# A fused mLSTM, soft mixture and routed mixture: a new order of the opening, three routed tiles planned early instead of two, and a new order between the mixtures

## The chip, the core and the metric

The kernel runs on one core of one Trainium2 chip. Its engines run side by side, each through its own instructions in order: TensorE (PE; PEld is its weight loads), VectorE (DVE), ScalarE (ACT), GpSimd (POOL) and SyncE (SP), whose queue issues most of the DMAs. An instruction waits until its operands are there; everything behind it on its engine waits with it. The metric is the device time of one execution in microseconds (us), lower is better.

## What is computed

From the reference, cut: a recurrent attention (q, k, v of 2 batches, 8 heads, 768 steps, head size 40), a soft mixture of 8 experts over its 1536 output tokens, and a second mixture in which each token goes to one expert.

```python
m_new = np.maximum(f_gate[:, :, t] + m, i_gate[:, :, t])      # for each step t
C = f_stab * C + i_stab * np.einsum('bhd,bhe->bhde', vt, kt)
n = f_stab * n + i_stab * kt
y[:, :, t] = sigmoid(o_gate) * np.einsum('bhde,bhe->bhd', C, qt) / np.maximum(np.abs(nq), 1.0)
...
P = np.exp(logits - logits.max())                              # first mixture: 8 rounds of row and
for e in range(E):                                             # column normalisation of P, then
    out += P[:, e:e + 1] * (np.maximum(x @ w1[e], 0.0) @ w2[e])
...
expert_idx = np.argmax(x @ w_gate, axis=1)                     # second mixture: one expert a token
out[mask] = gate_w[mask, None] * (np.maximum(xe @ w1[e], 0.0) @ w2[e])
```

## The kernel before

The 1536 tokens are 12 token tiles of 128. Precision is kept by splitting each operand into a rounded part and a rest (`xh` and `xl`, `w1h` and `w1l`, `w2h` and `w2l`, `hh` and `hl`), so a product takes two or three matmuls; the split is a cast on ScalarE and a subtraction on VectorE or GpSimd.

The order of the work is written out by hand. `attn(i)` is a generator that emits the attention of token tile i in steps. In the **opening** (from line 985) a list of `steps(...)` interleaves the first two, `f0` and `f1`, with `g1`, the gates of the second chunk of 128 steps (`gates`, ten small VectorE operations in a row, lines 143 to 167). `make_R` builds on VectorE the operand `R` that a tile's gate matmul (line 238) needs. `split_chunk` splits the first mixture's weights, six chunks an expert, from a ring of four buffers (`raw`). `keep_warm(n)` issues n matmuls on a dummy tile. The gate results on their way to weights `W` go through ScalarE and, for one half, VectorE (line 241); line 269 multiplies the scores into `W`. The finished tile x is turned by TensorE (`transpose_x`, lines 345 and 346).

Then `moe1` runs the first mixture item by item (`ITEMS`: token tiles, expert). Stage 1 of an item has eight **units** (`s1_unit`, lines 484 to 492, eight matmuls; the first item has two token tiles, 256 columns, the later ones 512), each closed by `hh` on ScalarE (line 493) and the subtraction `hl` on VectorE (line 494). Stage 2 is lines 499 to 501. After every half unit and every quarter of a token tile's stage 2 `bg` is called, and emits a step of each generator that is active: while the first five items run, `bg_early` feeds in the attention of the other ten token tiles, their gates (`GT`) and decays (`DT`), by the counter u.

While the last expert runs, `route(t)` finds token tile t's experts (logits on TensorE, line 606; one-hot matrix `ol` on VectorE, line 616; counts on TensorE, line 623) and scatters its rows by expert into a DRAM table (`rows`, line 629, a DMA of the GpSimd queue). The **second mixture** works on 128-row tiles of one expert. The first NE = 2 of them are planned by `early(k)` on VectorE before all tokens are routed: the expert with the most rows so far, of the first 8 + k token tiles; their rows are fetched by `gather` (line 780, GpSimd queue). After the last route `static_index` plans one tile an expert and `extra_plan` the rest. 17 tiles run; two more stand behind a branch at line 965, taken if more are needed. `moe2_tiles` runs tile j's stage 1 (`m2_s1`, line 864), its turned hidden layer (`m2_ht`, line 877), the turned x of tile j+1 (`m2_x`, line 345) and stage 2 of tile j-1 (line 904 and lines 499 to 501), and splits tile j+1's weights; after each piece it calls `tick`, which takes one step of `late`, the rest of routing and planning. The first tile (`lead`) has GpSimd for one of its splits.

Of the kernel before, what the change touches and what calls it, by code (L numbers as in the profile page):

```python
# [18 lines left out]
def mlstm_moe_moe_kernel(ctx, tc, q, k, v, i_gate, f_gate, o_gate, wg1, w1a, w2a, wg2, w1b, w2b, out):  # L19
# [15 lines left out]
    def f32(ap):  # L35
        return ap.bitcast(F32)
# [175 lines left out]
    def attn(i, ps=pst, lead=False):  # L212
# [242 lines left out]

    def split_chunk(eng=None, hi=None):
        n = nsplit[0]
        if n >= len(chunks):
            return
        e, w, t = chunks[n]  # L460
        if eng is None:
            eng = dve if e < 3 else pool
        r = raws.pop(n)
        if w == "w1":
            if hi is None:
                act.copy(out=w1h[:, t, :], in_=r)  # L466
            else:
                hi.tensor_copy(w1h[:, t, :], r)
            eng.tensor_tensor(out=w1l[:, t, :], in0=r, in1=f32(w1h[:, t, :]), op=ALU.subtract)  # L469
        else:  # L470
            k0, k1 = 3 * t, min(3 * t + 3, NF)
            rv = r[:, 0:(k1 - k0) * DM].rearrange("p (k d) -> p k d", d=DM)
            act.copy(out=w2h[:, k0:k1, :], in_=rv)
            eng.tensor_tensor(out=w2l[:, k0:k1, :], in0=rv, in1=f32(w2h[:, k0:k1, :]), op=ALU.subtract)
        nsplit[0] += 1
        load_chunk()

# [70 lines left out]

    NE = 2
    NX = NT - NE - 1  # L550
# [42 lines left out]
    def route(t):  # L593

        px = pst()
        for k in range(2):
            pe.transpose(px[:, k * L:(k + 1) * L], acc[:, t, k * L:(k + 1) * L], ident)
        pe.transpose(px[0:64, 2 * L:3 * L], acc[:, t, 256:DM], ident)
        xt = ro.tile([128, 3 * L], F32, tag="xt", name="xt")
        act.copy(out=xt[:, 0:2 * L], in_=px[:, 0:2 * L])  # L600
        act.copy(out=xt[0:64, 2 * L:], in_=px[0:64, 2 * L:3 * L])
        yield
        pl = pst()
        for k in range(3):
            n = 128 if k < 2 else 64
            pe.matmul(pl[:, 0:E], xt[0:n, k * L:(k + 1) * L], wgr2[0:n, k, :], start=(k == 0), stop=(k == 2))
        sm = ro2.tile([128, 4], F32, tag="sm", name="sm")
# [5 lines left out]
        act.activation(out=ex, in_=sh, func=AF.Exp)  # L613
        dve.scalar_tensor_tensor(out=sh, in0=sh, scalar=0.0, in1=ioe, op0=ALU.is_equal, op1=ALU.mult)
        dve.tensor_reduce(out=sm[:, 1:2], in_=sh, axis=AX.X, op=ALU.min)
        dve.tensor_scalar(out=ol[:, 0:E], in0=ioe, scalar1=sm[:, 1:2], scalar2=None, op0=ALU.is_equal)
# [290 lines left out]
    def moe2_tiles(lo, hi, tick, first=False):  # L907


        for j in range(lo, hi + 1):  # L910
# [22 lines left out]
            if new:  # L933
                m2_ht(j, 0)
# [49 lines left out]
    with tc.manual_schedule():  # L984
# [43 lines left out]
        steps(f1)  # L1028
        steps(g1)
        steps(f0)  # L1030
        steps(g1, g1)
        split_chunk()
        steps(f1, f1, f1)
        steps(f1)
        split_chunk()
        steps(f0)
        steps(g1, g1)
        steps(f1)
        drain(g1)
        make_R(2)  # L1040
        split_chunk()
        load_tile(3, "o")
        active = [f0, f1]
        GT = {0: 2, 10: 3, 20: 4, 30: 5}
        DT = {2: (1, 2), 15: (2, 3), 28: (3, 4), 44: (4, NCH)}

        slow = []

        def bg_early(u):
# [10 lines left out]
            if u == 8:  # L1060
                load_rows(wgr, wg1)
                sp.dma_start(out=wgr2[:, 0:2], in_=wg2[0:256, :].rearrange("(a p) f -> p a f", p=128))
                sp.dma_start(out=wgr2[0:64, 2], in_=wg2[256:320, :])
# [21 lines left out]
        def bg_main(n, u):  # L1085
# [24 lines left out]
            if e == E - 1 and u >= 2 * NF and u % 4 == 3:  # L1110
                q.append((units[0] + 3, route(t0 + (u - 2 * NF) // 4)))
            for k, (due, g) in enumerate(list(q)):
                if units[0] >= due:
                    q[k] = (units[0] + 2, g) if next(g, "end") != "end" else None
# [24 lines left out]
        def late():  # L1139
            gs = [g for _, g in st["q"]]  # L1140
            while True:
                gs = [g for g in gs if next(g, "end") != "end"]
                if not gs:
                    return
                yield
# [29 lines left out]
```

## Time and profile before

| | us |
|---|---|
| median of 3 runs (lowest, highest) | 1016.23 (1015.3, 1016.56) |
| the profiled execution | 1011.56 |
| its span, first to last instruction | 1009.4 |
| TensorE busy | 972.3 |
| mean granted TensorE clock, share of full speed | 0.983 |

The profiled execution is 2.16 us longer than its span, and 4.67 us under the median. Line numbers are those of the kernel before; in rows of the changed kernel they are its own, shifted by up to three.

### The profile page before, as it was taken

Reading aid. Unit: us, or ns where it says so; the run is one execution under the profiler, and the core shown is the slowest. Engines: PE = TensorE matmul, PEld = TensorE weight load, DVE = VectorE, ACT = ScalarE, POOL = GpSimd, SP = SyncE. Lnnn points to the kernel's source line nnn. Section 1 sums busy time; section 2 is a strip of 40 time slices with the busy share of each in tenths; the row PEclk is TensorE's granted clock in tenths of the full one; section 3 lists DMA queues with packets and bytes.
Section 4 is the critical chain, followed back from the end, with each engine's and each line's share of the span. In section 5 each row is a group of like instructions: output and inputs, shape, how many; then the busy total and the mean of one; then the engine's idle time right before and its main releaser. Section 6 shows DMA issues by size and latency. Waiting matters only on the chain. (4 is left out here: it accounts for less than half of the span.)

```text
span 1009.4 us, 14465 instructions
## 1 busy us (share of the span) xinstructions
PE 972.3 (96%) x5631; PEld 859.8 (85%) x5631; DVE 508.1 (50%) x1109; ACT 347.0 (34%) x578; POOL 216.9 (21%) x212
## 2 busy tenths in 40 slices
PE   7889999999999999999999999999999987999997
PEld 5788889788999988899998888999988976778885
DVE  7798978673523322222222222222235548887774
ACT  4535544322312232113113211311232124667772
POOL 3122312000000022005002200500221133655552
PEclk8799999999999999999999999999999998999999
DMA  9643531300321415002101200300100025788872
GB/s 182 146 78 45 112 71 55 103 1 1 97 102 54 145 33 196 12 1 75 41 1 54 62 1 1 97 19 1 33 1 27 21 86 148 205 233 241 242 231 81
DMA packets 91366, 84.11 MB, mean 83 GB/s; under 512 B 54237, under 2 KB 81887, under 8 KB 91296
## 3 DMA queue, kind: packets, MB, share of 16 engines
q1 hardware_dynamic: 89088, 76.42, 28.9%
q0 software_dynamic: 2208, 6.75, 1.9%
q8 instruction: 45, 0.74, 0.3%
q14 instruction: 25, 0.20, 0.1%
HBM read 79.21 MB, written 4.76 MB: 83 GB/s over the span
## 5 line engine op out<-in xcount | busy, mean ns | idle before, releaser
L493 ACT ACTIVATE hh<-s 128x512 fp32r<-128x512 f32 (+1 forms) x200 | 116.7, 583 | 451.3 <-PE s L492 451.0
L499 PE MATMUL s<-w2h,hh 128*128 128x320 f32 x836 | 263.4, 315 | 0.0
L501 PE MATMUL s<-w2h,hl 128*128 128x320 f32 x836 | 259.1, 310 | 0.0
L500 PE MATMUL s<-w2l,hh 128*128 128x320 f32 x836 | 259.1, 310 | 0.0
L494 DVE SCALAR_TENSOR_TENSOR hl<-s,hh 128x512 fp32r<-128x512 f32 (+1 forms) x200 | 133.5, 668 | 213.4 <-ACT hh L493 213.0
L499 PEld LDWEIGHTS s<-w2h,hh 128*128 128x128 f32 x836 | 157.8, 189 | 2.3 <-issue 0.3
L500 PEld LDWEIGHTS s<-w2l,hh 128*128 128x128 f32 x836 | 157.8, 189 | 1.4 <-DVE w2l L847 0.2
L501 PEld LDWEIGHTS s<-w2h,hl 128*128 128x128 f32 x836 | 157.6, 189 | 0.0
L541 DVE SCALAR_TENSOR_TENSOR acc<-s,probs,acc 128x320 f32<-128x320 f32 x76 | 41.8, 550 | 191.9 <-PE s L501 191.9
L469 POOL TENSOR_TENSOR w1l<-raw,w1h 128x1024 fp32r<-128x1024 f32 x15 | 35.8, 2412 | 396.6 <-ACT w1h L466 396.6
L489 PE MATMUL s<-xl,w1h 128*128 128x512 f32 (+1 forms) x200 | 80.8, 404 | 0.0
L484 PE MATMUL s<-xh,w1h 128*128 128x512 f32 (+1 forms) x200 | 79.2, 396 | 1.6 <-DVE cbd L336 1.2
L486 PE MATMUL s<-xh,w1l 128*128 128x512 f32 (+1 forms) x200 | 77.9, 389 | 0.0
L491 PE MATMUL s<-xh,w1h 128*128 128x512 f32 (+1 forms) x200 | 77.9, 389 | 0.0
L485 PE MATMUL s<-xl,w1h 128*128 128x512 f32 (+1 forms) x200 | 77.1, 386 | 0.5 <-DVE xl L358 0.5
L490 PE MATMUL s<-xh,w1l 128*128 128x512 f32 (+1 forms) x200 | 77.2, 386 | 0.0
L492 PE MATMUL s<-xh,w1l 128*128 128x512 f32 (+1 forms) x200 | 77.2, 386 | 0.0
L487 PE MATMUL s<-xh,w1h 128*128 128x512 f32 (+1 forms) x200 | 77.1, 386 | 0.0
L830 POOL TENSOR_TENSOR w1l<-raw,w1h 128x1024 fp32r<-128x1024 f32 x16 | 45.5, 2846 | 30.7 <-ACT w1h L824 30.5
L484 PEld LDWEIGHTS s<-xh,w1h 128*128 128x128 f32 x200 | 37.9, 189 | 11.2 <-issue 1.9
L489 PEld LDWEIGHTS s<-xl,w1h 128*128 128x128 f32 x200 | 37.9, 189 | 8.9
L491 PEld LDWEIGHTS s<-xh,w1h 128*128 128x128 f32 x200 | 37.9, 189 | 8.7
(303 smaller groups left out, 1454.9 us busy)
## 6 DMA issues: line engine op xcount, KB each, us to landing
raw<-in_moe_w_dram SPq DMA_DIRECT2D x44, 320.0 KB, 3.4
raw<-in_moe_w_dram SPq DMA_DIRECT2D x54, 256.0 KB, 4.4
w2raw<-in_moe_w_dram SPq DMA_DIRECT2D x17, 640.0 KB, 5.2
raw<-in_moe_w_dram SPq DMA_DIRECT2D x20, 512.0 KB, 3.5
raw<-in_moe_w_dram SPq DMA_DIRECT2D x20, 480.0 KB, 4.1
wr<-in_moe_w_dram SPq DMA_DIRECT2D x8, 1024.0 KB, 8.6
q<-in_q_dram SPq DMA_DIRECT2D x12, 160.0 KB, 4.4
k<-in_k_dram SPq DMA_DIRECT2D x12, 160.0 KB, 4.6
```

The costliest lines, as they stand in the source:

```text
L484: pe.matmul(p, w1h[:, 0, fs], xh_[:, 0, cols], start=True, stop=False)
L485: pe.matmul(p, w1h[:, 0, fs], xl_[:, 0, cols], start=False, stop=False)
L486: pe.matmul(p, w1l[:, 0, fs], xh_[:, 0, cols], start=False, stop=False)
L489: pe.matmul(p, w1h[:, 1, fs], xl_[:, 1, cols], start=False, stop=False)
L490: pe.matmul(p, w1l[:, 1, fs], xh_[:, 1, cols], start=False, stop=False)
L491: pe.matmul(p, w1h[:, 2, fs], xh_[:, 2, cols], start=False, stop=False)
L492: pe.matmul(p, w1l[:, 2, fs], xh_[:, 2, cols], start=False, stop=True)
L493: act.activation(out=hh[:, ft, 0:n], in_=p, func=AF.Relu)
L494: dve.scalar_tensor_tensor(out=hl[:, ft, 0:n], in0=p, scalar=0.0, in1=f32(hh[:, ft, 0:n]), op0=ALU.max, op1=ALU.subtract)
L499: pe.matmul(p[:, 0:DM], hh[:, ft, ts], w2h[:, ft, :], start=(first and ft == 0), stop=False)
L500: pe.matmul(p[:, 0:DM], hh[:, ft, ts], w2l[:, ft, :], start=False, stop=False)
L501: pe.matmul(p[:, 0:DM], hl[:, ft, ts], w2h[:, ft, :], start=False, stop=(ft == NF - 1))
```

## The change

- **Opening.** The steps come in another order: no x is turned between the two tiles' last products, gates and `make_R(2)` move behind the first units of the first item, two `keep_warm(2)` come in, a third weight split moves into the item, and the attention of token tile 2 is started at u = 4 instead of u = 1. The first `w1h` cast goes from VectorE to ScalarE, two small copies of the sums from ScalarE to VectorE.
- **Plan.** NE is 3: a third tile is planned from the first ten token tiles, inside `late`; each expert's tile and the extra tiles follow, so 17 of 19 tiles run as before, with the branch taken if more than 6 extra tiles are needed (before: 7).
- **Between the mixtures.** `early(0)` comes two half units earlier and in closer steps; the first routed tile's weight splits come earlier and go from GpSimd to VectorE, as do the lead tile's; the lead tile's `m2_ht` and `m2_x` come before stage 1 of the second; the last two token tiles are routed in a written order. `route` copies its turned x in one piece.

```diff
@@ attn
         if lead:
-            act.copy(out=nq, in_=pv[:, :, D:V])
+            dve.tensor_copy(nq, pv[:, :, D:V])
...
         yield
-        if lead:
-            transpose_x(x, i, ps, act)
-            yield
         if c < NCH - 1:
             pc = ps()
...
-            transpose_x(x, i, ps)
-            yield
+        transpose_x(x, i, ps, act if lead else None)
+        yield
@@ moe1, NE, route, early, split2_w1l
-                if newe and ft < 3 or n == 0 and ft in (3, 5):
+                if newe and ft < 3 or n == 0 and ft in (1, 3, 5):
                     split_chunk()
...
-    NE = 2
+    NE = 3
...
-        act.copy(out=xt[:, 0:2 * L], in_=px[:, 0:2 * L])
-        act.copy(out=xt[0:64, 2 * L:], in_=px[0:64, 2 * L:3 * L])
+        act.copy(out=xt, in_=px[:, 0:3 * L])
...
-    SP1 = 2 * (DM + 4)
+    SP1 = NE * (DM + 4)
...
-            load2(j + 1, 0)
+            if j > 0:
+                load2(j + 1, 0)
@@ moe2_tiles
-                split2_w1l(j + 1, 1, pool if lead else None)
+                split2_w1l(j + 1, 1)
+            if lead:
+                m2_ht(j, 0)
+                m2_x(j + 1)
+            if nxt:
                 split2_w1h(j + 1, 2)
-                split2_w1l(j + 1, 2, dve if lead else None)
-            if lead:
-                m2_x(j + 1)
+                split2_w1l(j + 1, 2, dve if first and j <= lo + 1 else None)
@@ the opening
         steps(f0, f0, f1, f0, f1)
-        steps(f0, f0, f0)
-        steps(g1, g1, g1)
+        steps(f0, g1, g1)
         steps(f1)
-        steps(f0)
-        steps(f1, f1, f1)
-        split_chunk(dve, dve)
+        steps(f0, f0)
+        steps(f1, f1)
+        steps(g1, g1)
+        low = split_chunk(wait=True)
...
         keep_warm(3)
         steps(f0, f0, f0)
         steps(f1)
-        steps(g1)
+        low()
         steps(f0)
-        steps(g1, g1)
+        keep_warm(2)
+        steps(f1, f1, f1)
+        steps(f0)
+        steps(f1)
+        low = split_chunk(wait=True)
+        steps(f0)
+        steps(f1)
+        steps(f1)
+        low()
         split_chunk()
...
-        drain(g1)
-        make_R(2)
-        split_chunk()
+        keep_warm(2)
         load_tile(3, "o")
-        active = [f0, f1]
-        GT = {0: 2, 10: 3, 20: 4, 30: 5}
-        DT = {2: (1, 2), 15: (2, 3), 28: (3, 4), 44: (4, NCH)}
+        active = [g1, g1]
+        GT = {4: 2, 12: 3, 20: 4, 30: 5}
+        DT = {6: (1, 2), 15: (2, 3), 28: (3, 4), 44: (4, NCH)}
...
+            if u == 3:
+                active.extend((f0, f1))
+                make_R(2)
-            if u % 8 == 1 and u // 8 + 2 < NT:
+            if (u == 4 or u % 8 == 1 and u > 1) and u // 8 + 2 < NT:
@@ the last item, late
-            if last and u in (9, 26):
+            if last and u in (7, 26):
                 g = early(u // 26)
                 next(g)
-                q.append((units[0] + 1, g))
-            if last and u in (17, 20, 26):
-                split2_w1h(0, (u - 17) // 3 if u < 26 else 2)
-                split2_w1l(0, (u - 17) // 3 if u < 26 else 2, pool)
+                q.append((units[0] + 1, g, 1))
+            if last and u in (17, 18, 19):
+                split2_w1h(0, u - 17)
+                split2_w1l(0, u - 17, dve if u == 19 else None)
+            if last and u == 27:
+                load2(1, 0)
...
+            a, b = [g for _, g, _ in st["q"]][-2:]
+            c = early(2)
+            for gs in ((a,), (b,), (c,), (a, c), (c,), (b,), (), (b,)):
+                for g in gs:
+                    next(g)
                 yield
```

What VectorE has in its queue early in the opening, before and after (`a` and `s` are PSUM tiles, `acc` holds the gates here):

```order
 L241 TENSOR_SCALAR W<-a 128x512
 L224 COPY kT<-s_272 128x512
-L269 TENSOR_TENSOR W<-a,W 128x4x128 x2
 L148 SCALAR_TENSOR_TENSOR acc<-acc 16x128
 L151 TENSOR_TENSOR acc<-acc 16x128
+L241 TENSOR_SCALAR W<-s_296 128x512
+L269 TENSOR_TENSOR W<-a,W 128x4x128 x2
 L153 TENSOR_TENSOR acc<-acc 16x128
-L241 TENSOR_SCALAR W<-s_301 128x512
```

The second tile's line 241 now stands ahead of the first tile's line 269.

On TensorE, the first unit of the first mixture before the change, with what stands around it:

```order
L346 MATMUL s_402<-ident,x 64x128
L317 MATMUL a<-v_99,ku_97 128x82 x4
L317 MATMUL s_421<-v_100,ku_98 128x82 x4
L484 MATMUL s_435<-xh_65,w1h 128x256
L485 MATMUL s_435<-xl_68,w1h 128x256
L486 MATMUL s_435<-xh_65,w1l 128x256
L487 MATMUL s_435<-xh_65,w1h 128x256
L489 MATMUL s_435<-xl_68,w1h 128x256
L490 MATMUL s_435<-xh_65,w1l 128x256
L491 MATMUL s_435<-xh_65,w1h 128x256
L492 MATMUL s_435<-xh_65,w1l 128x256
L238 MATMUL a<-R,gl__110 128x512 x2
```

and the third unit after it:

```order
L483 MATMUL s_461<-xh_65,w1h 128x256
L484 MATMUL s_461<-xl_68,w1h 128x256
L485 MATMUL s_461<-xh_65,w1l 128x256
L486 MATMUL s_461<-xh_65,w1h 128x256
L238 MATMUL a<-R,gl__110 128x512 x2
L488 MATMUL s_461<-xl_68,w1h 128x256
L489 MATMUL s_461<-xh_65,w1l 128x256
L490 MATMUL s_461<-xh_65,w1h 128x256
L491 MATMUL s_461<-xh_65,w1l 128x256
L222 MATMUL a<-ident,q_93 128x128 x4
```

Token tile 2's gate matmul (line 238) moved from behind the first unit into the middle of the third.

VectorE around the one-hot matrix `ol` of the last routed token tile, between the mixtures, before:

```order
L638 TENSOR_TENSOR tab<-bt 128x8
L611 TENSOR_REDUCE sm<-a 128x1
L612 TENSOR_SCALAR sh<-a,sm 128x8
L614 SCALAR_TENSOR_TENSOR sh<-sh,ioe 128x8
L615 TENSOR_REDUCE sm<-sh 128x1
L616 TENSOR_SCALAR ol<-ioe,sm 128x8
```

and after (lines 672 to 677 end the plan of the third early tile):

```order
L886 TENSOR_TENSOR hl<-a,hh 128x4x128
L672 TENSOR_TENSOR es<-acc,io 128x1
L673 SCALAR_TENSOR_TENSOR acc<-acc,es 128x11
L674 TENSOR_REDUCE es<-acc 128x1
L675 SCALAR_TENSOR_TENSOR es<-es,acc 128x1
L640 TENSOR_SCALAR idx<-es 128x1
L677 SCALAR_TENSOR_TENSOR tab<-ed,tab 128x8
L608 TENSOR_REDUCE sm<-a 128x1
L609 TENSOR_SCALAR sh<-a,sm 128x8
L612 SCALAR_TENSOR_TENSOR hot<-sh,ioe 128x8
L613 TENSOR_REDUCE sm<-hot 128x1
L614 TENSOR_SCALAR ol<-ioe,sm 128x8
```

The plan of the third tile and, ahead of these rows, three weight splits and the split of x moved in front of the last route.

## Rows read from the trace of the kernel before

**Rows 1.** The page: TensorE's busy time, and its granted clock in 40 slices.

```profile
PE 972.3 (96%) x5631; PEld 859.8 (85%) x5631; DVE 508.1 (50%) x1109; ACT 347.0 (34%) x578; POOL 216.9 (21%) x212
...
PEclk8799999999999999999999999999999998999999
```

**Rows 2.** Windows of the opening: length, busy time (instructions) by engine, granted clock, DMA.

```profile
10.62:61.43 50.81, 39.74 (x268) 35.35 (x267) 37.94 (x85) 22.46 (x45) 9.29 (x18) 0.80 0.86 152
16.00:19.30 3.30, 3.30 (x18) 2.85 (x17) 2.92 (x4) 2.76 (x4) 0.96 (x3) 0.50 1.44 143
22.60:39.90 17.30, 14.32 (x71) 12.99 (x69) 11.38 (x28) 8.07 (x16) 2.24 (x4) 0.51 0.96 189
61.40:185.00 123.60, 117.34 (x875) 106.50 (x874) 105.88 (x215) 58.37 (x112) 28.11 (x42) 1.00 0.36 71
```

**Rows 3.** TensorE's waits in the first 62 us: total, times, longest.

```profile
PE s L261 <- DVE W L241: 3.0, 1, 3.0
PE a L345 <- DVE x L305: 1.7, 1, 1.7
```

**Rows 4.** Timeline of VectorE in the opening: start, us, operation.

```profile
14.01 0.67 DVE L241 TENSOR_SCALAR W<-s 128x512 f32<-128x512 f32 x1
...
32.77 1.23 DVE L208 TENSOR_TENSOR R<-gx,mask 128x1024 fp32r<-128x1024 f32 x1
...
61.04 0.39 DVE L494 SCALAR_TENSOR_TENSOR hl<-s,hh 128x256 fp32r<-128x256 f32 x1
```

**Rows 5.** TensorE's waits from 805 to 870 us.

```profile
PE a L623 <- DVE ol L616: 3.3, 2, 2.0
PE a L345 <- DMA acc<-rows,idx: 2.5, 1, 2.5
PE s L864 <- DVE xl L358: 2.3, 2, 1.2
PE s L864 <- POOL w1l L834: 1.6, 1, 1.6
```

**Rows 6.** Windows between the mixtures, columns as in rows 2.

```profile
821.00:824.70 3.70, 3.06 (x12) 3.05 (x13) 0.99 (x3) 1.32 (x2) 0.76 (x1) 0.58 0.00 0
835.60:838.60 3.00, 0.96 (x10) 0.77 (x9) 2.42 (x13) 0.21 (x1) 0.00 (x0) 1.00 0.73 231
838.60:842.00 3.40, 3.40 (x12) 2.93 (x11) 3.19 (x14) 1.88 (x4) 1.04 (x1) 0.50 0.16 45
```

**Rows 7.** Window of line 492 alone (once a unit), columns as rows 2.

```profile
807.00:812.60 5.60, 1.18 (x3) 0.57 (x4) 1.00 0.09 32
```

**Rows 8.** Timeline of all engines at 833 us.

```profile
833.13 2.38 POOL L830 TENSOR_TENSOR w1l<-raw,w1h 128x1024 fp32r<-128x1024 f32 x1
833.39 2.14 DVE L670 TENSOR_SCALAR ed<-ioe,es 128x8 f32<-128x8 f32 x1
```

**Rows 9.** Windows of VectorE's planning and routing work, columns as in rows 2.

```profile
810.62:814.46 3.84, 3.48 (x15) 2.53 (x14) 3.49 (x17) 1.20 (x2) 0.00 (x0) 1.00 0.19 37
829.08:831.12 2.04, 2.04 (x17) 1.94 (x18) 1.46 (x9) 0.21 (x1) 0.00 (x0) 1.00 0.00 0
```

**Rows 10.** Operations on the tile w1l, 790 to 880 us (ns min/median/max).

```profile
L834 DVE TENSOR_TENSOR w1l<-wr,w1h x7: 1214/1216/3584, 848.9 to 878.8; 128x1024 fp32r<-128x1024 f32 x7
```

**Rows 11.** The gathers of line 780: issue on GpSimd (ns min/median/max), landing.

```profile
L780 POOL DMA_INDIRECT acc<-rows,idx x17: 1016/1142/1567, 815.2 to 973.9; - x17
...
DMA to landing us min/median/max: 3.0/3.9/6.3
```

**Rows 12.** DMA issues by line: count, KB each, median us to landing.

```profile
w2raw<-in_moe_w_dram SPq DMA_DIRECT2D x17, 640.0 KB, 5.2
...
rows<-acc,slot POOLq DMA_INDIRECT x12, 2.7
```

**Rows 13.** Timeline of TensorE, one routed tile to the next.

```profile
868.58 2.31 PE L904 MATMUL s<-w2raw,hraw 128*128 128x320 f32 x8
...
877.36 2.31 PE L904 MATMUL s<-w2raw,hraw 128*128 128x320 f32 x8
```

More of the change, by code (lines that the diff above doesn't have):

```diff
@@ L454, in load_chunk, with split_chunk @@
         nload[0] += 1
-    def split_chunk(eng=None, hi=None):
+    def split_chunk(eng=None, wait=False):
         n = nsplit[0]
@@ L464, in split_chunk, with low @@
         if w == "w1":
[L465 to L469, printed above, removed]
+            rv, h, l = r, w1h[:, t, :], w1l[:, t, :]
         else:
             k0, k1 = 3 * t, min(3 * t + 3, NF)
-            rv = r[:, 0:(k1 - k0) * DM].rearrange("p (k d) -> p k d", d=DM)
-            act.copy(out=w2h[:, k0:k1, :], in_=rv)
-            eng.tensor_tensor(out=w2l[:, k0:k1, :], in0=rv, in1=f32(w2h[:, k0:k1, :]), op=ALU.subtract)
+            rv, h, l = r[:, 0:(k1 - k0) * DM].rearrange("p (k d) -> p k d", d=DM), w2h[:, k0:k1, :], w2l[:, k0:k1, :]
+        act.copy(out=h, in_=rv)
         nsplit[0] += 1
-        load_chunk()
+        def low():
+            eng.tensor_tensor(out=l, in0=rv, in1=f32(h), op=ALU.subtract)
+            load_chunk()
+        if wait:
+            return low
+        low()
     def s1_unit(t0, nt, ft, mid):
@@ L597, in route @@
             pe.transpose(px[:, k * L:(k + 1) * L], acc[:, t, k * L:(k + 1) * L], ident)
-        pe.transpose(px[0:64, 2 * L:3 * L], acc[:, t, 256:DM], ident)
+        pe.transpose(px[:, 2 * L:3 * L], acc[:, t, DM - L:DM], ident)
         xt = ro.tile([128, 3 * L], F32, tag="xt", name="xt")
-        act.copy(out=xt[:, 0:2 * L], in_=px[:, 0:2 * L])
-        act.copy(out=xt[0:64, 2 * L:], in_=px[0:64, 2 * L:3 * L])
+        act.copy(out=xt, in_=px[:, 0:3 * L])
         yield
@@ L604, in route @@
         for k in range(3):
-            n = 128 if k < 2 else 64
-            pe.matmul(pl[:, 0:E], xt[0:n, k * L:(k + 1) * L], wgr2[0:n, k, :], start=(k == 0), stop=(k == 2))
+            pe.matmul(pl[:, 0:E], xt[:, k * L:(k + 1) * L], wgr2[:, k, :], start=(k == 0), stop=(k == 2))
         sm = ro2.tile([128, 4], F32, tag="sm", name="sm")
@@ L613, in route @@
         act.activation(out=ex, in_=sh, func=AF.Exp)
-        dve.scalar_tensor_tensor(out=sh, in0=sh, scalar=0.0, in1=ioe, op0=ALU.is_equal, op1=ALU.mult)
-        dve.tensor_reduce(out=sm[:, 1:2], in_=sh, axis=AX.X, op=ALU.min)
+        hot = ro2.tile([128, E], F32, tag="hot", name="hot")
+        dve.scalar_tensor_tensor(out=hot, in0=sh, scalar=0.0, in1=ioe, op0=ALU.is_equal, op1=ALU.mult)
+        dve.tensor_reduce(out=sm[:, 1:2], in_=hot, axis=AX.X, op=ALU.min)
         dve.tensor_scalar(out=ol[:, 0:E], in0=ioe, scalar1=sm[:, 1:2], scalar2=None, op0=ALU.is_equal)
@@ L932, in moe2_tiles @@
                 m2_s2(j - 1, p, 0)
-            if new:
+            if new and not lead:
                 m2_ht(j, 0)
@@ L1028, in mlstm_moe_moe_kernel @@
         steps(f1)
-        steps(g1)
+        low()
         steps(f0)
-        steps(g1, g1)
-        split_chunk()
-        steps(f1, f1, f1)
-        steps(f1)
-        split_chunk()
-        steps(f0)
-        steps(g1, g1)
-        steps(f1)
-        drain(g1)
-        make_R(2)
-        split_chunk()
+        keep_warm(2)
[6 more added lines that the diff above has]
+        steps(f1)
+        low()
+        split_chunk()
+        keep_warm(2)
         load_tile(3, "o")
-        active = [f0, f1]
-        GT = {0: 2, 10: 3, 20: 4, 30: 5}
-        DT = {2: (1, 2), 15: (2, 3), 28: (3, 4), 44: (4, NCH)}
+        active = [g1, g1]
+        GT = {4: 2, 12: 3, 20: 4, 30: 5}
+        DT = {6: (1, 2), 15: (2, 3), 28: (3, 4), 44: (4, NCH)}
         slow = []
@@ L1062, in bg_early @@
                 sp.dma_start(out=wgr2[:, 0:2], in_=wg2[0:256, :].rearrange("(a p) f -> p a f", p=128))
-                sp.dma_start(out=wgr2[0:64, 2], in_=wg2[256:320, :])
+                dve.memset(wgr2[0:64, 2], 0.0)
+                sp.dma_start(out=wgr2[64:128, 2], in_=wg2[256:320, :])
             if u == 20:
                 split_wg()
-            if u % 8 == 1 and u // 8 + 2 < NT:
+            if u == 3:
+                active.extend((f0, f1))
+                make_R(2)
+            if (u == 4 or u % 8 == 1 and u > 1) and u // 8 + 2 < NT:
                 g = attn(u // 8 + 2)
@@ L1110, in bg_main @@
             if e == E - 1 and u >= 2 * NF and u % 4 == 3:
-                q.append((units[0] + 3, route(t0 + (u - 2 * NF) // 4)))
-            for k, (due, g) in enumerate(list(q)):
+                q.append((units[0] + 3, route(t0 + (u - 2 * NF) // 4), 2))
+            for k, (due, g, every) in enumerate(list(q)):
                 if units[0] >= due:
-                    q[k] = (units[0] + 2, g) if next(g, "end") != "end" else None
+                    q[k] = (units[0] + every, g, every) if next(g, "end") != "end" else None
             q[:] = [x for x in q if x]
-            if last and u in (9, 26):
+            if last and u in (7, 26):
                 g = early(u // 26)
                 next(g)
-                q.append((units[0] + 1, g))
-            if last and u in (17, 20, 26):
-                split2_w1h(0, (u - 17) // 3 if u < 26 else 2)
-                split2_w1l(0, (u - 17) // 3 if u < 26 else 2, pool)
+                q.append((units[0] + 1, g, 1))
[4 more added lines that the diff above has]
+                load2(1, 0)
             if last and u > 29:
@@ L1139, in late @@
         def late():
[L1140 to L1144, printed above, removed]
+            a, b = [g for _, g, _ in st["q"]][-2:]
[3 more added lines that the diff above has]
+                    next(g)
                 yield
```

## The prediction

> **What bounds the kernel now.** I read the page first. TensorE is busy for 972.3 of 1009.4 us, and its granted clock is below full only in the first two slices of the span and in one or two near 830 us [rows 1]. Between these two places the change moves nothing that TensorE waits for, so what it can win lies in the opening and between the mixtures, and what it wins there reaches the end of the run as long as TensorE stays the bound behind it.
>
> The opening, by windows: from 16.0 to 19.3 us and from 22.6 to 39.9 us TensorE ran at half clock (0.50 and 0.51; 1.2 of 2.4 GHz), and it was busy for 14.32 of the 17.3 us of the second stretch [rows 2]. TensorE's waits show what went before: 3.0 us at the scores of the second tile (line 261) for VectorE's line 241, then 1.7 us for the finished x (line 345) [rows 3]. The timeline says why the first was long: line 241 started at 14.01 us [rows 4], and the order of the queue puts line 269 of the first tile ahead of it, which has to wait for the masked weights of GpSimd. The reader is to see that VectorE's queue, not its speed, is late: from 10.62 us to 61.43 us, the end of the eighth unit's subtraction [rows 2, 4], VectorE was busy for 37.94 of 50.81 us, so 12.87 us idle, while TensorE waited for it or crawled. Behind that, from 61.4 to 185 us, TensorE was busy for 117.34 of 123.6 us at full clock and VectorE for 105.88 [rows 2]: the first is the bound, the second is not far from it.
>
> Between the mixtures, by waits: 2.5 us for the first gather, 3.3 us in two waits for `ol` (the longest 2.0), 2.3 us in two for `xl`, 1.6 us for a weight split of GpSimd [rows 5]. After the first and after the 2.0 the clock fell: 0.58 from 821 to 824.7 us, 0.50 from 838.6 to 842 us [rows 6].
>
> **The opening, step by step.** The change puts line 241 of the second tile ahead of line 269. It could start when TensorE's gate matmul is done, about 2.5 us earlier; the 3.0 us shrink to a few tenths, and with them goes the fall of the clock behind them. No x is turned between the two products, so the 1.7 us wait has `keep_warm` and the state products (line 317) in its place. Gates, `make_R(2)` and the attention of token tile 2 stand behind the first units, so the first unit needs only its weight splits and can start near 22 us.
>
> From there VectorE sets the pace, and I sum its queue, not TensorE's. Up to the eighth unit's subtraction it holds the old list with six operations fewer (the cast that ScalarE takes, the three of token tile 2's x, two of the gates) and three very small ones more. At the stretch's mean of 0.45 us (37.94 / 85 [rows 2]) that is about 2 us less, of which all but the cast, say 1.3 us, is only postponed. So it needs 36 us behind 10.62 us, plus its idle time. That can't be nothing: it must wait for the second tile's sums and for x to be turned twice (about 1.5 us together, estimated by following both queues). It need not be the old 12.87, since what caused most of that is moved; I take 5 us, because of a new wait: line 238 of token tile 2 now stands in the middle of the third unit and needs `make_R(2)`, 1.23 us on VectorE [rows 4], which is queued behind two weight splits, four gate operations, two subtractions and a `w2l` split. TensorE comes there some 3 us early; all that is behind line 238 waits, the rest of the third unit and the turning of q and k. After such a wait the clock fell before [rows 2, 3], so I expect a stretch at half clock here too, shorter than the old 17.3 us. The eighth subtraction then ends at 10.62 + 36 + 5 = 51.6 us instead of 61.43; 9.8 us, less the 1.3 postponed, is 8.5, and I keep **8 us** for the opening. The bounds: idle 1.5 us gives 12; idle 9.5 gives 4. TensorE does not overrule this: its 39.74 us of work in the stretch contain 3.3 + 14.3 at half clock [rows 2], so about 31 at full.
>
> The added copies, the `keep_warm(2)` and the memset of `wgr2` I cost at nothing: the copies take the place of ScalarE's on the same path, and the warm matmuls lie in waits of TensorE for VectorE; if those waits are gone they cost their own few tenths. The load queue keeps its order but for two swaps, and the weights it brings are needed only in stage 2.
>
> **Between the mixtures.** *First gather.* Its index is written one unit earlier in VectorE's queue; a unit takes 5.60 / 3 = 1.87 us [rows 7]. That leaves 0.6 of the 2.5 us: +1.9. *The first `ol`.* VectorE's line 670 took 2.14 us beside a split on GpSimd of 2.38 us that had begun 0.26 us before it [rows 8]; seventeen operations of the same plan took 3.49 us elsewhere [rows 9], 0.2 each. The change takes the split to VectorE and to an earlier place, so the delay of 1.9 us goes; TensorE arrives earlier too, so I count 1.2 of the 2.0. *The clock.* Without these two waits the stretches at half clock go: 3.06 us at 0.58 and 3.40 at 0.50 [rows 6] cost 1.3 + 1.7 = 3.0. *The GpSimd split* of the lead tile (1.6 us wait [rows 5]) goes to VectorE at 1.22 us [rows 10], where it is hidden: +1.6. Together 7.7.
>
> Against it: before the last route's `ol` VectorE now has three splits (3 x 1.22 [rows 10]), the plan of the third tile with a subtraction (3.84 us [rows 9]), nine short operations (about 1.8 at 0.2) and the route's own 1.5 of 2.04 us [rows 9], 10.8 us in all, starting 2.0 us after the logits of token tile 10. TensorE comes there after 26 matmuls of 512 columns (1.87 / 8 = 0.23 each), fourteen transposes and one set of logits, about 8.5 us, and some 2 us of waits for the hidden layer and `xl`. So it waits 12.8 - 10.5, about 2.5 us, where the second `ol` wait was 1.3: -1.2. Behind it stand stage 2 of the first routed tile and the x of the third. After 2.0 us the clock fell last time; half of that price, -0.8, is my middle between nothing and 1.7. *The third gather* is new on the path: its index is written in that same chain, a gather lands after 3.0 to 6.3 us, median 3.9 [rows 11], and each scatter of `rows` (2.7 us [rows 12]) and each gather waits for the one before in the table. By the median it lands about when TensorE turns its x; by the longest, 2.4 us late. The fourth is in the same position one tile later. I take -0.7 for both; the bounds are 0 and -5. That leaves 7.7 - 1.2 - 0.8 - 0.7 = **5 us**, bounds 0 and 8.
>
> Here a page is weighed. The trace shows one direction of a conflict: VectorE's operation stretched by a GpSimd split that began first [rows 8]; gathers were issued in 1.02 to 1.57 us [rows 11], so anything that held them cost at most 0.55 us. The Trainium skill, SBUF — State Buffer, section Who interferes with whom, says that VectorE and GpSimd share a port pair as an exclusive lock, in which the one that starts first blocks the other for its whole instruction, and that a VectorE operation with two SBUF inputs contends with reads of GpSimd. That speaks against moving splits to VectorE next to gathers: by the rule each could hold a gather's issue for up to 1.22 us, and the sum would lose up to 2.4 more on the third and fourth gather. By the rows it is 1.1 at most, which lies within my bound.
>
> **The sum.** 8 + 5 = 13 us. The profiled execution of 1011.56 us would become 998.6; it lies 4.67 us under the median of the runs, which I take to stay, so 1016.2 - 13 = **1003.2 us**. A difference of 0.2% (2 us) is about what a measurement of this kernel can tell from none.
>
> **Rivals.**
> - *The opening's lead is given back.* VectorE was busy for 105.88 of 123.6 us until 185 us [rows 2], and token tile 2's attention now falls closer to tile 3's. If its lateness makes TensorE wait there, about 5 of the 8 us go: 1008. For it: small slack. Against: the old idle time of 17.7 us there.
> - *Nothing is won between the mixtures.* The waits change places: the third and fourth gather land at their longest and the clock falls twice. 1016.2 - 8 = 1008. The Trainium skill's lock would work on this side. Against: no split runs on GpSimd there any more.
> - *Both*: 1013.
> - *The change doesn't do what it says*: the wait at line 238 takes the clock down until 40 us again, and TensorE is no earlier at stage 2; with the rival above, 1015 to 1017.
> - *Slower: the branch runs.* 17 tiles ran, by the loads of `w2raw` [rows 12]. With 11 instead of 10 tiles fixed, more than 6 extra tiles open the branch. Two more tiles cost 2 x 8.78 us [rows 13] and a cold start of their weights, 5.2 us at least [rows 12]: 1003 + 23 = 1026. It decides if the third early tile's expert needed no further extra tile. Against it: counting the routing of the reference's inputs gives 7 extra tiles with two early ones and 6 with three.
>
> **Chances.** Forecast 0.52 (998 to 1007 by the bounds of its terms); more than that, near 996, 0.05; opening given back 0.16; nothing between the mixtures 0.13; both 0.06; does nothing 0.05; slower 0.03. From these: faster 0.88 (half of "both" and "nothing" may fall within 0.2%, the rest is above), same 0.07, slower 0.05. The range that leaves out less than 2 in 10 is 996 to 1013.
>
> **What would show it.** Right: the first unit's line 484 near 22 us, the eighth unit's subtraction near 52 us, at least half of the stretch to 40 us at full clock; the wait for the first gather under 1 us, no VectorE operation of 2 us beside a GpSimd split at 833, one wait of 2 to 3 us for the last `ol`. Wrong: a granted clock of 0.5 past 40 us; TensorE's waits for VectorE between 61 and 185 us growing beyond the present 6 us; waits of 2 us and more for the third or fourth gather; loads of `w2raw` beyond 17.

## The result

The changed kernel takes 1005.11 us, the median of four runs (1004.0 to 1005.49), beside 1015.76 of the kernel before in the same set (1013.97 to 1016.56): a ratio of 0.9888, 95% interval 0.9855 to 0.992. Timed once more it took 1004.07 us beside 1015.54, 0.9877 (0.9849 to 0.9905). Forecast was 1003.2. The profiled execution took 1005.28 us, and of before 1011.56: the two profiles show only 6.3 of the 10.65 us, a gap that the experiments take up.

The page of after, its span, busy times and granted clock in 40 slices, beside [rows 1]:

```profile
span 1003.6 us, 14464 instructions
...
PE 969.0 (97%) x5633; PEld 856.1 (85%) x5635; DVE 512.6 (51%) x1130; ACT 346.4 (35%) x565; POOL 204.7 (20%) x207
...
PEclk9897999999999999999999999999999999999999
```

TensorE is still the bound. The clock is below full at the start, and now in the fourth slice too (75 to 100 us), where it was full before.

The opening by windows up to the end of the eighth subtraction, and two stretches in it; columns as in [rows 2]:

```profile
core 0: us, PE busy (x) PEld busy (x) DVE busy (x) ACT busy (x) POOL busy (x), PEclk, DMA share, GB/s
10.62:54.70 44.08, 35.18 (x271) 31.30 (x270) 35.95 (x83) 22.86 (x44) 8.82 (x16) 0.92 0.79 165
...
30.00:33.00 3.00, 2.74 (x11) 2.55 (x12) 1.74 (x6) 1.88 (x4) 0.60 (x1) 0.56 1.01 290
...
40.00:43.00 3.00, 2.95 (x16) 2.71 (x15) 2.28 (x5) 2.80 (x7) 1.27 (x2) 0.60 1.06 178
```

TensorE's waits in the opening of after, beside [rows 3]:

```profile
engine line waited for: us in total, times, longest us
PE a L238 <- DVE R L208: 3.0, 1, 3.0
PE a L238 <- DVE wgr L1064: 1.9, 1, 1.9
PE a L314 <- DVE num L298: 1.1, 1, 1.1
...
PE s L261 <- DVE W L241: 0.7, 1, 0.7
```

And VectorE's timeline there, beside [rows 4]; behind an operation stand its idle time and what ended it:

```profile
27.93 1.15 DVE L471 TENSOR_TENSOR w2l<-raw,w2h 128x960 fp32r<-128x960 f32 x1
28.99 1.22 DVE L208 TENSOR_TENSOR R<-gx,mask 128x1024 fp32r<-128x1024 f32 x1
...
33.77 0.42 DVE L493 SCALAR_TENSOR_TENSOR hl<-s,hh 128x256 fp32r<-128x256 f32 x1 [1.94 <-ACT hh L492]
...
37.92 1.19 DVE L208 TENSOR_TENSOR R<-gx,mask 128x1024 fp32r<-128x1024 f32 x1
...
43.46 0.42 DVE L493 SCALAR_TENSOR_TENSOR hl<-s,hh 128x256 fp32r<-128x256 f32 x1 [1.18 <-ACT hh L492]
...
47.50 0.42 DVE L493 SCALAR_TENSOR_TENSOR hl<-s,hh 128x256 fp32r<-128x256 f32 x1 [1.12 <-ACT hh L492]
...
54.31 0.41 DVE L493 SCALAR_TENSOR_TENSOR hl<-s,hh 128x256 fp32r<-128x256 f32 x1
```

The 3.0 us at line 261 are 0.7, and the new wait at line 238 is 3.0, behind line 208, as forecast. It comes a second time one token tile later (1.9 us). The row names the memset of `wgr2` there (line 1064), which ended 0.02 us behind the next line 208 (39.13 and 39.11 us); e1, which has no memset, shows the same wait for line 208 (2.18 us). Behind each the clock is down for some 3 to 4 us, and VectorE in turn waits for units that TensorE finished late (1.94, 1.18 and 1.12 us).

TensorE's waits between the mixtures, 785 to 900 us, beside [rows 5]:

```profile
PE s L863 <- DVE xl L355: 2.8, 2, 2.5
PE a L876 <- ACT acc L865: 1.8, 1, 1.8
PE a L621 <- DVE ol L614: 1.6, 1, 1.6
PE a L342 <- DMA acc<-rows,idx: 1.4, 2, 0.9
```

The 2.5 us for the first gather are 0.5, one of the two waits for `ol` is gone and so is that for GpSimd's split. The clock stays full from 785 to 866 us in this execution.

How far each execution is at the same place is seen in the start of the activation of `hh` (line 492 of after), counted through the first mixture. From the timelines, in us; the last column is the time from the last activation to the end of the span, and the experiments e1 to f4 are described below:

| profiled execution | 1st | 9th | 17th | 185th | last (200th) to the end |
|---|---|---|---|---|---|
| before | 34.05 | 74.54 | 117.38 | 766.16 | 193.8 |
| before, again (f3) | 35.12 | 75.52 | 118.35 | 767.19 | 198.6 |
| after | 25.64 | 69.60 | 117.58 | 766.03 | 189.1 |
| after, again (e9) | 25.69 | 70.46 | 116.81 | 765.24 | 188.4 |
| opening alone (e1) | 25.51 | 69.87 | 113.13 | 761.98 | 196.1 |
| between alone (e2) | 35.12 | 75.55 | 118.39 | 766.83 | 189.3 |
| after, e4 | 25.49 | 70.79 | 114.00 | 762.45 | 189.1 |
| after, e5 | 25.51 | 68.54 | 111.74 | 760.19 | 188.5 |
| after, e6 | 25.17 | 69.11 | 114.28 | 762.72 | 189.4 |
| after, e8 | 25.49 | 69.53 | 115.91 | 764.17 | 186.4 |
| after, f2 | 25.63 | 68.17 | 111.35 | 759.82 | 189.7 |
| after, f4 | 25.49 | 69.44 | 117.46 | 765.86 | 189.8 |
| before, e7 | 29.85 | 73.14 | 119.17 | 768.03 | 195.2 |
| before, f1 | 36.39 | 77.79 | 122.76 | 771.65 | 193.2 |

After's profiled execution wins 8.4 us up to the first activation and 4.9 up to the ninth, loses them before the seventeenth, and gains 5.7 of its 5.8 us of span behind the 185th. The first profile of before flatters it at the ninth: it is the earliest of the four with before's opening and no added matmuls there (before, f3, e2, f1: mean 75.9 us), and the eight with after's opening unchanged up to there (after, e9, e1, e4, e5, e6, e8, f4) have a mean of 69.7, so the lead there is 6.2 us by the means. Where after lost its lead, by windows of after:

```profile
82.00:84.00 2.00, 0.32 (x3) 0.35 (x3) 1.89 (x7) 0.00 (x0) 0.00 (x0) 1.00 1.04 180
84.00:86.00 2.00, 2.00 (x13) 1.89 (x13) 1.97 (x5) 1.00 (x4) 0.00 (x0) 0.75 0.08 15
86.00:88.00 2.00, 2.00 (x10) 1.81 (x9) 1.97 (x4) 1.03 (x2) 0.00 (x0) 0.50 0.00 0
...
92.00:94.00 2.00, 2.00 (x12) 2.00 (x11) 1.18 (x3) 0.04 (x1) 0.77 (x2) 0.50 0.00 0
```

TensorE waited 1.88 us there for VectorE's line 355, ahead of the transposes of line 184, and ran at 0.50 for about 10 us behind it. In before's profile it waits 1.86 us at the same instruction, and the clock stays at 1.00. The instruction in after, then in before, and a window of before behind it:

```profile
83.69 0.20 PE L184 MATMUL a<-ident,acc 16*128 16x16 f32 x1 [1.88 <-DVE xl L355]
```

```profile
88.25 0.20 PE L184 MATMUL a<-ident,acc 16*128 16x16 f32 x1 [1.86 <-DVE xl L358]
```

```profile
90.00:92.00 2.00, 2.00 (x18) 1.91 (x17) 1.94 (x5) 1.41 (x4) 0.00 (x0) 1.00 0.00 0
```

### The profile page after: what moved, and what is told of

Same layout as the page of the kernel before. It is cut to its first block, busy times and chain, and to the rows that moved or that the text cites. A ratio compares the mean times of both kernels' runs of the same rounds, so it can differ in the third digit from the quotient of the medians.

```text
span 1003.6 us, 14464 instructions
## 1 busy us (share of the span) xinstructions
PE 969.0 (97%) x5633; PEld 856.1 (85%) x5635; DVE 512.6 (51%) x1130; ACT 346.4 (35%) x565; POOL 204.7 (20%) x207
## 5 line engine op out<-in xcount | busy, mean ns | idle before, releaser
L471 POOL TENSOR_TENSOR w1l<-raw,w1h 128x1024 fp32r<-128x1024 f32 x15 | 35.8, 2419 | 396.5 <-ACT w1h L467 396.5
L833 DVE TENSOR_TENSOR w1l<-wr,w1h 128x1024 fp32r<-128x1024 f32 x34 | 45.9, 1352 | 1.3 <-ACT w1h L824 1.2
L483 PEld LDWEIGHTS s<-xh,w1h 128*128 128x128 f32 x200 | 38.1, 191 | 9.7 <-DVE hl L493 1.0
L491 PEld LDWEIGHTS s<-xh,w1l 128*128 128x128 f32 x200 | 38.0, 190 | 9.4 <-DVE w1l L471 0.8
L489 PEld LDWEIGHTS s<-xh,w1l 128*128 128x128 f32 x200 | 38.0, 190 | 8.8 <-DVE w1l L471 1.0
```

Source lines behind the costliest of these rows:

```text
L483: pe.matmul(p, w1h[:, 0, fs], xh_[:, 0, cols], start=True, stop=False)
L489: pe.matmul(p, w1l[:, 1, fs], xh_[:, 1, cols], start=False, stop=False)
L491: pe.matmul(p, w1l[:, 2, fs], xh_[:, 2, cols], start=False, stop=True)
```

## The experiments

Times stand beside runs of the kernel before on the same chip: medians 1015.89 for e1 to e5, 1015.54 for e6 to e9, 1016.53 for f1 to f4.

**The two halves apart.** The change touches two places that share no code. In e1 the opening's edits alone were made to the kernel before; e2 has all the others. One line of each edit:

```diff
 e1: -        GT = {0: 2, 10: 3, 20: 4, 30: 5}
 e1: +        GT = {4: 2, 12: 3, 20: 4, 30: 5}
 e2: -    NE = 2
 e2: +    NE = 3
```

e1: 

> The opening's part of the change alone; two early tiles and the order between the mixtures as before. Theory of the prediction: the opening is worth 8 us, so about 1008 beside 1015.8 of before. Rival, from the profile after: the lead of 4.6 us that the opening wins is lost again behind a wait of 1.9 us near 84 us, after which the clock stood at 0.50 for some 10 us; by it this kernel is within 3 us of before, 1013 to 1016, with first units as early as after (line 483 near 22 us).

e2: 

> The part between the mixtures alone; the opening as before. Theory of the prediction: worth 5 us, about 1011. Rival, from the two profiles, in which this part was worth about 6 us and the opening nothing at the end: if all of the 10.65 us come from here, 1005. The waits behind the first gather and the first ol under 1 us in both.

e1 took 1009.34 us, 0.9941 (0.9915 to 0.9967), or 6.0 us less; e2 1008.83, 0.9942 (0.9918 to 0.9965), or 5.9 us less. Together that is 11.9 by the ratios, beside 11.4 and 12.5 of the whole in its two sets (10.65 and 11.47 between the medians). Both halves pay; the rivals by which one of them brings nothing fall. The profiles say the same: behind the last activation, the eight with the new order between the mixtures (without e8) take 188.4 to 189.8 us, the five with the old one 193.2 to 198.6. e1 kept its lead in its profile (4.2 us at the 185th activation), with the clock full from 36 to 816 us.

**The lead that after lost.** e4 puts eight matmuls on a constant tile into the wait ahead of line 184, e9 is after once more:

```diff
-    def decays(c0, c1):
+    def decays(c0, c1, w=0):
...
+        if w:
+            wp = ps2()
+            for _ in range(w):
+                pe.matmul(wp, warm[:, 0:128], warm, start=True, stop=True)
         p = pst()
...
-        DT = {6: (1, 2), 15: (2, 3), 28: (3, 4), 44: (4, NCH)}
+        DT = {6: (1, 2), 15: (2, 3), 28: (3, 4, 8), 44: (4, NCH)}
```

e4: 

> The changed kernel with eight matmuls on a constant tile, whose result nobody reads, put into the wait of 1.9 us ahead of the transposes of line 184 near 82 us; the same instructions on VectorE. If that wait is what takes the clock down afterwards, and the fall what takes the opening's lead: full clock from 84 to 98 us, the lead of 4.6 us kept to the end, 1000 to 1001.5 instead of 1005.1. Rival: the clock falls at another place or the lead is lost to VectorE's queue anyway: 1004 to 1006.

e9: 

> The changed kernel once more, for its spread and a second profile. If the half clock from 85 to 96 us belongs to the kernel, it is there again, and the times stay at 1004 to 1005.5. If it is a matter of the execution, the second profile has it elsewhere or not at all, and the times spread by 4 us and more, as those of the kernel before do (1012.4 to 1019.7).

e4 took 1000.99 us (999.5 to 1001.82, four runs), below every one of the ten runs of after (1002.48 to 1005.49). Its windows at the place:

```profile
82.00:84.00 2.00, 2.00 (x15) 1.37 (x15) 1.95 (x5) 0.76 (x2) 0.00 (x0) 1.00 1.07 189
84.00:86.00 2.00, 1.87 (x13) 1.19 (x11) 1.90 (x5) 0.26 (x2) 0.00 (x0) 1.00 0.72 124
86.00:88.00 2.00, 2.00 (x17) 1.91 (x17) 1.94 (x5) 1.37 (x4) 0.00 (x0) 1.00 0.00 0
```

The lead at the 185th activation is 3.7 us. e9's second profile of after had the half clock again (86 to 93 us), and so had f4's and e8's (e8, whose opening is that of after, is described below). But e5 has the opening of after, the same wait of 1.9 us, and no fall:

```profile
80.00:82.00 2.00, 0.77 (x7) 0.56 (x5) 1.95 (x5) 0.62 (x2) 0.00 (x0) 1.00 1.15 200
82.00:84.00 2.00, 1.36 (x11) 1.28 (x11) 1.92 (x5) 0.49 (x3) 0.00 (x0) 1.00 0.56 94
84.00:86.00 2.00, 2.00 (x18) 1.92 (x18) 1.94 (x5) 1.40 (x4) 0.00 (x0) 1.00 0.00 0
```

So the fall is a matter of the execution, which this order meets often: four of the six profiles with the wait as after has it, e1's and e5's being the two without. Before's order can meet it too, as e7 below shows. That the fall costs after some 3 to 4 us (1005.11 and 1004.07 against 1000.99) is shown by e4; what decides it stays open.

**Clock or VectorE's queue in the opening.** e7 leaves before's order and fills its waits with idle matmuls, f1 fills only the wait ahead of line 184 in before, with e4's edit. The edits of e7, cut:

```diff
 e7: +            fill(8, pst)
              transpose_x(x, i, ps, act)
...
 e7: +        fill(12, pst)
          steps(f1, f1, f1)
...
 e7: +            if u < 10:
 e7: +                fill(2, ps2)
```

e7: 

> The kernel before, its order unchanged, with idle matmuls of 512 columns in TensorE's waits of the opening: twelve ahead of the second tile's scores, eight ahead of each of the two turns of x, two at each of the first ten steps beside stage 1. Theory of the prediction, VectorE's queue sets the pace of the opening: full clock, but no gain, 1014 to 1018. Rival, drawn from the first four kernels, where the times at an equal mean clock put the opening's order at only 1.4 us: the opening's 6 us come by the clock, so most of them are won here too, 1010 to 1012.

f1: 

> The kernel before with nothing but the eight idle matmuls in its wait of 1.9 us ahead of line 184 (near 86 us). In the profile shown of before this wait was followed by full clock, yet its timed runs lie about 4 us higher. If that is because in most executions the clock does fall there, as it did in two profiles of the changed kernel: 1011.5 to 1012.5, and the runs above 1015 gone. Rival: the timed runs of before are slower for another reason: 1015 to 1016, no change.

e7 took 1012.46 us, 0.9962 (0.9938 to 0.9986), 3.9 us less by the ratio: between the two expectations. With full clock up to 34 us the old order reaches the first activation 4.2 us earlier, the new order 8.4. As far as the idle matmuls cost nothing there, about half of the opening's lead at that place is thus the order itself, beyond the clock that it keeps. Of e7's 4.2 us 1.4 are left at the ninth; behind that its profile (1014.85 us, longer than its median) has half clock from 89 to 95 us, behind the same wait of 1.86 us at line 184 that before's profile passed at full clock. How much of the opening's 6.0 us at the end of the run is order and how much clock is not settled: the intervals of e1 (3.4 to 8.6) and e7 (1.4 to 6.3) overlap.

f1 took 1014.66, 0.9982 (0.9959 to 1.0004): no change that can be told. By itself that doesn't refute the theory that before's timed runs lie above its profile because of that wait: f1's profile has full clock behind the filled wait, but half clock from 106 to 113 us behind the next one, 1.21 us ahead of the product with `W` (line 280 of before), and from 15 to 45 us. f3, below, speaks against it.

f2 has the edits of e4 and e5 (below) and fills after's two waits at line 238 as well:

```diff
+        if i in (2, 3):
+            wp = ps2()
+            for _ in range(13 if i == 2 else 8):
+                pe.matmul(wp, warm[:, 0:128], warm, start=True, stop=True)
```

f2: 

> The kernel with both edits (idle matmuls ahead of line 184, the split on VectorE) and more idle matmuls in the two waits at line 238 in the opening: thirteen near 27 us, eight near 37 us. If TensorE at half clock behind these waits (some 7 us at 0.50 to 0.67) sets the pace: 3 us less, about 997.5, and the range of the runs narrower. If VectorE's queue sets it, as the prediction has it: full clock there, the eighth subtraction no earlier, 1000 to 1001.

f2 took 1000.95 us (999.67 to 1012.95), e6, the same without these fills, 1000.54. Its opening by windows:

```profile
10.62:53.29 42.67, 36.57 (x291) 30.20 (x290) 36.04 (x83) 22.67 (x44) 8.81 (x16) 1.00 0.79 169
30.00:33.00 3.00, 2.83 (x23) 2.66 (x22) 1.74 (x6) 2.09 (x4) 0.64 (x1) 1.00 1.17 298
```

At full clock throughout, the eighth subtraction ends at 53.29 us instead of 54.70: the two stretches at half clock cost 1.4 us there, and nothing that the runs can tell. The rest of VectorE's time is there with the clock full: 36.04 us of work and 6.6 idle.

**Where before loses more than its profile showed.** f3 is before, unchanged:

> The kernel before, unchanged, for a second profile. By the theory of the falling clock a time near 1016 shows half clock for some 10 us behind the wait near 86 us, and a time near 1012 does not.

It took 1017.49 us in one run, with full clock behind line 184: a long execution without the fall that the theory wants. Its last activation of the first mixture is 1.0 us later than in the first profile of before; the other 4.9 of the 5.9 us lie between the mixtures. TensorE's waits there, GpSimd's timeline and a window of f3:

```profile
PE s L864 <- POOL w1l L834: 5.3, 1, 5.3
PE a L623 <- DVE ol L616: 3.2, 2, 2.0
```

```profile
852.55 1.63 POOL L629 DMA_INDIRECT rows<-acc,slot  x1 [6.88 <-DVE tab L638]
858.27 1.07 POOL L629 DMA_INDIRECT rows<-acc,slot  x1 [4.09 <-DMA rows<-acc,slot]
859.35 2.36 POOL L834 TENSOR_TENSOR w1l<-wr,w1h 128x1024 fp32r<-128x1024 f32 x1
```

```profile
860.00:867.00 7.00, 5.23 (x11) 3.83 (x12) 1.82 (x2) 2.58 (x3) 4.80 (x4) 0.51 0.20 63
```

The split of the lead tile is queued on GpSimd behind a scatter of `rows` that waits for the scatter before it to land. When that one is late, TensorE waits 5.3 us for the split instead of 1.6 [rows 5], and runs at half clock behind. The change took this split off GpSimd, and no profile of after or e2 has the wait. The others that keep it there show 3.0 us (e1), 3.7 (e7) and 1.5 (f1). Nor is this the only place: f1's execution of 1016.50 us is 5.5 us behind before's first profile at the 185th activation already.

**VectorE and GpSimd between the mixtures.** Two operations beside each other on the timelines of after's VectorE and GpSimd:

```profile
859.28 1.21 DVE L833 TENSOR_TENSOR w1l<-wr,w1h 128x1024 fp32r<-128x1024 f32 x1
859.42 1.99 POOL L778 DMA_INDIRECT acc<-rows,idx  x1 [0.30 <-issue]
861.29 3.63 DVE L833 TENSOR_TENSOR w1l<-wr,w1h 128x1024 fp32r<-128x1024 f32 x1
861.43 2.40 POOL L828 TENSOR_TENSOR w1l<-raw,w1h 128x1024 fp32r<-128x1024 f32 x1
```

The two splits of line 833 are VectorE's; the second took 3.63 us, its usual 1.21 and GpSimd's 2.40 added; TensorE's 2.5 us for `xl` and a stretch at 0.50 to 0.66 (866 to 870 us) are behind it. e5 moves that split of GpSimd, f4 the one of the first routed tile the other way:

```diff
 e5: -                split2_w1l(j + 1, 2, dve if first and j <= lo + 1 else None)
 e5: +                split2_w1l(j + 1, 2, dve if first and j <= lo + 2 else None)
 f4: -                split2_w1l(0, u - 17, dve if u == 19 else None)
 f4: +                split2_w1l(0, u - 17, pool if u == 19 else None)
```

e5: 

> The changed kernel with the third of the three low halves of the fourth routed tile's first weights, the one next to which a VectorE operation of line 833 took 3.63 us instead of 1.22, moved from GpSimd to VectorE too. If the two engines hold each other up there: that operation 1.2 us, TensorE's wait for xl of 2.5 us down to 1.3 or less, no half clock behind it, 1002 to 1003. Rival: VectorE is only busier by 1.2 us and the wait stays, 1005 to 1006.

f4: 

> The changed kernel with the one split of the first routed tile (u == 19) back on GpSimd at its new place. The prediction gives the move to VectorE 1.2 us, for a line of VectorE's plan that took 2.14 us beside that split, and 1.7 more for the clock behind the wait: 1006 to 1007.5. Rival: at its earlier place the split lies beside no plan, and where it runs doesn't matter: 1004 to 1005.5.

e5 took 1001.59 us (997.84 to 1004.77). TensorE's waits, 785 to 880 us:

```profile
PE a L342 <- DMA acc<-rows,idx: 4.5, 2, 3.5
PE a L876 <- ACT acc L865: 1.9, 1, 1.9
PE a L621 <- DVE ol L614: 1.6, 1, 1.6
PE s L863 <- DVE xl L355: 0.7, 2, 0.3
```

The 2.5 us for `xl` are gone, but TensorE waits 3.5 us for the third tile's gather (0.9 in after). This gather and the VectorE split beside it, in after and then in e5:

```profile
848.35 1.05 POOL L778 DMA_INDIRECT acc<-rows,idx  x1 [3.90 <-DVE acc L618]
848.41 1.23 DVE L833 TENSOR_TENSOR w1l<-wr,w1h 128x1024 fp32r<-128x1024 f32 x1 [0.44 <-ACT w1h L824]
```

```profile
843.19 1.23 DVE L833 TENSOR_TENSOR w1l<-wr,w1h 128x1024 fp32r<-128x1024 f32 x1 [0.44 <-ACT w1h L824]
843.30 2.04 POOL L778 DMA_INDIRECT acc<-rows,idx  x1 [4.05 <-DVE acc L618]
```

Where the gather's record begins 0.06 us ahead of the split's, it is issued in 1.05 us; where it begins 0.08 to 0.14 us behind (e4, e5, e6, f2), in 2.01 to 2.07. TensorE's wait for it is 3.4 to 3.6 us in e5, e6 and f2 and at most 1.3 in e4, so the issue alone doesn't make it. e5's profile, the fastest of all at 998.89, is 6.4 us shorter than after's, and 5.8 of them lie ahead of the 185th activation, where the clock did not fall. What the move itself is worth is not settled: the runs of e5 overlap those of after. f4 took 1004.32 us (1000.9 to 1006.36), as after, and the first `ol` wait is gone there too: where that split runs makes no difference that can be told at its new place, beside no plan.

**Both edits.** e6 has those of e4 and e5.

> The two edits together: the eight idle matmuls in the wait ahead of line 184, and the fourth routed tile's last split on VectorE. If each removes a fall of the clock of its own: 1005.1 - 4.1 - 3.5, about 997.5. Rival: which waits are followed by a fall changes from execution to execution, so that the one is worth less where the other is done: 999 to 1001.

It took 1000.54 us (997.02 to 1003.5), 0.9837 (0.9804 to 0.987). Its profile has full clock near 84 us and half clock from 98 to 105 us instead, behind a wait of 1.2 us ahead of the product with `W` (line 280 of after). So the rival is right, as f1's profile says too: with one wait filled, the clock can fall behind another. It is the lowest ratio here, but its interval overlaps that of after.

**The third early tile by itself.** e8 is the changed kernel with NE back at 2; expected were 1002.4 us by the prediction's sum, and 1007 to 1010 by a rival. It took 1000.98 us (999.45 to 1001.5), but its output is wrong, so this time is no price of the third tile. What that tile brings or costs alone is not shown, nor what the other edits between the mixtures bring one by one, beyond e5 and f4.

## Why the prediction was right, and where it was not

- **The start of the opening.** The wait at line 261 (0.7 us, forecast a few tenths), the first unit (line 483 at 21.90 us, forecast near 22), the new wait at line 238 (2.99 us, forecast some 3) and a shorter stretch at half clock came as worked out.
- **VectorE's sum.** Its work up to the eighth subtraction was 35.95 us; forecast 36. Its idle time was 44.08 - 35.95 = 8.1 us; forecast 5. This is the term that was mis-sized: 54.70 us instead of 51.6. Of its 5 us the prediction gave 1.5 to the second tile's sums and x, and so 3.5 to the wait at line 238. By windows, 2.2 us of the idle time lie ahead of 26.06 us, 3.1 from there to 36.20, around that wait, and 2.9 behind it. So the new wait was sized about right and taken to come once; it came again with the next `make_R`. f2 puts the clock's share of the miss at 1.4 us.
- **What was postponed.** The lead was 8.4 us at the first activation, 6.7 at the eighth subtraction ([rows 4] against 54.31 us) and 4.9 at the ninth activation: 1.8 lost in between, where the forecast had 1.3 postponed. That the 1.8 are the postponed work is argued, not shown. In e1's runs the opening is worth 6.0 us (3.4 to 8.6) where 8 were forecast.
- **The lead given back.** The rival had it by TensorE waiting more for VectorE up to 185 us. Those waits are the same as before (4.0 us from 62 to 190 us), as the prediction's first paragraph held; it is the clock behind one of them, which was full in the profile of before. The rival had 16 in 100; in four of six profiles the lead over before's first profile was lost in whole or in great part by the 185th activation, by a mechanism that the prediction didn't have.
- **Between the mixtures.** 5.9 us (3.6 to 8.3); forecast 5. In the profile: first gather 0.5 us (1.3 in e9; forecast 0.6), the two half-clock stretches [rows 6] gone, last `ol` 1.6 (forecast 2.5, though 12.8 - 10.5 is 2.3), no fall of the clock behind it (forecast 0.8 us), the third gather 0.9 (1.0 in e9, 3.5 in e5; forecast 0.7 for two). The first `ol` came right for half of a reason: f4 shows that the earlier place of the split did it, and the engine made no difference. GpSimd's split was taken at the 1.6 us of one execution; f3 and e1 show 5.3 and 3.0.
- **What the sum left out.** The wait for the hidden layer, 1.8 us and not there before, and the waits for `xl`, 2.8 us (2.3 before), stand in the prediction only as "some 2 us" in the dating of TensorE's arrival; no term of the sum takes them off. In e9 the clock falls behind the first of them, as in e4; in after it doesn't:

```profile
839.11 0.66 PE L876 MATMUL a<-ident,acc 128*128 128x128 f32 x4 [1.88 <-ACT acc L865]
```

```profile
842.00:844.00 2.00, 2.00 (x7) 1.61 (x7) 1.86 (x9) 0.09 (x1) 0.40 (x1) 0.50 0.69 172
```

  That 5 us came out near 5.9 is thus in part luck: a term at nothing (these waits) and one too small (GpSimd's split) worked against each other.
- **The conflict that was weighed.** The rows gave 0.55 us at most for holding a gather's issue. In after one gather, the fifth, was held by 1.99 - 1.04 = 0.95 us:

```profile
L778 POOL DMA_INDIRECT acc<-rows,idx x17: 1043/1172/1990, 812.2 to 967.7; - x17
```

  The rule of the Trainium skill (SBUF — State Buffer, Who interferes with whom) allowed up to 1.22, and agrees better: the held gather began 0.14 us behind the split, when 1.07 us of the split were left. By the rows, though, VectorE's operation of 3.63 us began first and still waited for the whole of GpSimd's, which the rule's first-come order doesn't give. That the third gather, on which the sum had a term, was not held in after is luck by 0.06 us; in e4, e5, e6 and f2 it was. The rival's "no split runs on GpSimd there any more" is wrong: one runs at 861.43 us. And [rows 10] had the sign of the second conflict: its longest split, 3.58 us at 860.67, lay beside GpSimd's 2.41 from 860.75 us in before; the prediction put every split at 1.22.
- **The sum.** The 13 us were made of 8 and 5 and came as 6.0 and 5.9, together 11.4 and 12.5 by the ratios of the whole. That the profile of before lies under its median was taken as a fixed offset; it is not one, since f3 shows that a longer execution of before holds waits which the change removes.
- **The branch.** 17 loads of `w2raw`, as before; it did not run.

## What to carry to other kernels

Where one engine's queue sets the pace, sum its work and then ask, for each wait of the engine it feeds, what the first one has left to do meanwhile: the idle time comes back. A wait of 1 to 2 us of TensorE that is followed by full clock in one profile may be followed by 7 to 10 us at half clock in the next; count such waits, and take several profiles before calling one harmless. Work that stands on GpSimd behind a scatter which waits for another scatter has a start that varies: by 4 us between the two profiles of before, counted from the last activation. Look for a queue without such a wait.

## What was not expected of the hardware

The runs of before spread from 1011.29 to 1023.1 us, and their mean granted clocks from 0.983 to 0.969 with them: a time says little without its clock. At the same instruction, behind the same 1.9 us of waiting, the clock fell in some executions and not in others; from the ninth to the seventeenth activation after, e9, f4 and e8, with the fall, took 5.1, 3.5, 5.2 and 3.5 us more than the first profile of before, and e5 and e1, without it, 0.4. A VectorE split that met one of GpSimd took both durations, 3.63 us; whether a gather of 1.05 us takes 2.04 hung on 0.1 us between two records.
